# A Strassen down product, with weights stationary, in an RWKV-7 and MLP kernel

## The chip, the cores and the metric

The kernel runs on one core of one Trainium2 chip. The metric is the device time of one execution in microseconds (us). TensorE (PE) does the matmuls, VectorE (DVE), ScalarE (ACT) and GpSimd (POOL) the elementwise work, and SyncE (SP) issues all DMAs. Everything is float32.

## The reference

A recurrence over 768 steps for 4 batches and 8 heads of 40 channels, and behind it an MLP over the 3072 tokens:

```python
for t in range(S):                                   # S = 768, state is 40 x 40 for each (batch, head)
    y[:, :, t] = einsum('bhd,bhde->bhe', rt, state)
    Sa = einsum('bhde,bhe->bhd', state, at)
    state = state * wt[:, :, None, :] - einsum('bhd,bhe->bhde', Sa, bt) + einsum('bhd,bhe->bhde', vt, kt)
x = y.transpose(0, 2, 1, 3).reshape(3072, 320)
h = x @ w_in                                         # 320 x 2048
g = h * (1.0 / (1.0 + exp(-1.702 * h)))
out = g @ w_out                                      # 2048 x 320
```

## The kernel before

**The recurrence.** Time is cut into 12 chunks of 64 steps. A *unit* is one chunk of one pair of batches, so there are 24 units, and units 2c and 2c+1 make up chunk c. For each unit the kernel loads its tiles (`load`, `load_w`), forms decays (`decay`), scales the inputs and forms score products (`prep`: ps_A, ps_RV), inverts the triangular matrix of the chunk in levels (`inverse`: ps_N, ps_level, ps_Q, ps_T) and applies it to state and inputs (`solve`: ps_zT, ps_rz, ps_B, ps_X, ps_y). The last product of a unit is `read` (ps_y). From it come the new state and the output y, on VectorE, and then x = y times a decay (`decayed`, four steps on DVE or POOL). x goes to DRAM (`part_with`, x_dram<-x) and is read back in another layout, twice, into both halves of the partitions (`get_back`, xT_all<-x_dram). All of these DMAs are issued on SP, in the order of the list below.

**The MLP**, `mlp(c)`, works on the 256 tokens of one chunk. TensorE is used as four 64x64 tiles (`QUARTERS`), so four matmuls run at once; I call them a set. In the *up* product the weights are stationary and 256 tokens move: 40 sets for a chunk, eight groups of 256 features with 5 steps of 64 over the 320 inputs each. Four Gelus of 128x1024 (ACT) turn them into g. In the *down* product g is stationary and 320 columns of w_out move:

```python
for r, b in QUARTERS:
    o = p * 128 + b * 64
    mm(po[HALF[b], r, :DM], g[HALF[r], f % 2, o:o + 64], w_out_sb[HALF[r], f * DM:(f + 1) * DM], f == 0)
```

That is 32 sets for a chunk, in two accumulations of 128 tokens. Each one is copied to the tile ob (ACT or DVE), the sum of the other half of the rows is added (DVE), and two DMAs store 64 tokens each. w_in and w_out come as int64 bit patterns, 1.3 MB for each of eight pieces (`weight`), and are turned into floats on ACT, DVE and POOL (`joined`, 3 us each). `raws` says where the raw pieces stand before that: in the tile `extra`, in free parts of w_sb, or in the part of xT_all that chunks 1 and 2 use later.

**The order.** Nothing is scheduled by a tool at build time. The program makes a list of tasks with what each reads and writes (`plan.add`), and `ORDER`, a string, names each task by its number, with a letter for its engine (p, a, d, g, s) and a digit for its pair of PSUM banks. Every engine works through its tasks strictly in this order, and so does SP with the DMAs. A matmul that waits holds up all matmuls behind it. The figures in `plan.add`, such as `{"POOL": 730.0, "DVE": 434.0}`, are estimates that don't reach the chip. Line 300 is the helper `mm` that issues every matmul, so that in the profile matmuls are told apart by their tile.

**Buffers that matter here.** Tiles go round: `g` has four of 128 x 1024, xT_all has three chunks (`c % 3`), and all MLP and recurrence products share four pairs of PSUM banks.

Of the kernel before, what the change touches and what calls it, by code (L numbers as in the profile page):

```python
# [16 lines left out]
FP32 = mybir.dt.float32  # L17
# [89 lines left out]
ORDER = """  # L107
0s 8s 26s 5s 7s 9s 3a 6s 87p0 88p1 24s 89a1 1s 2s 12s 102a 95d 100p2 90a0 93d 158a 101d2 98p3 96g 10s 94d 17s 97g 16s 99d3
103p1 4a 11s 132p0 104a1 105d1 142p2 143p3 133a0 106d 130p1 14s 144a3 13s 107p0 15s 18s 151g 108a0 109d0 51s 131a1 110p3 27s
149g 150d 111a3 112d3 159p0 156p1 145a2 161d0 160a0 152g 113p3 345s 92a 162d 25s 153d 114a3 163p2 42s 115d3 34s 19a 274s 264p0  # L110
165d2 265p3 164a2 22d 266a3 166p2 20d 273s 21d 33s 43s 167a2 154p3 168d2 23g 35s 28a 157d1 116p2 155d3 169p1 117a2 118d2 267a0
279d 63s 280g 119p3 277s 171d1 36s 44s 123a3 120d3 343s 125d3 121a 278g 124d3 29d 287a 126p2 170a1 288p0 127a2 30d 172p1 479s
122a3 31d 289a0 128p2 54s 173a1 45s 129d2 32g 62s 174d1 134p3 37a 290d0 175p2 344s 135d3 180a2 146s 178a2 275s 176d2 136p1
179a2 38d 181a2 39d 177a 282g 276s 291d 91s 138a1 182p0 188p3 281d 183a0 186p2 139d 137a1 283p0 187a2 184p1 189a3 40d 140s
292p2 46a 60s 284d0 41g 285p3 185d1 148a 286d3 190p0 293a2 294d2 334p1 335p3 357a 191d0 141s 268g 147s 336a3 315d 192p2 47d
337a1 348d 316p0 194a2 346s 295p3 349d 61s 317a0 195g 347s 358p1 296a3 297d3 360d1 318a0 298p3 271a 361d 319p0 338g 300d3 196s
193a2 320a0 355p2 385d 270s 48d 299a3 362p0 356d2 351g 301p3 363a0 364d0 350g 386p2 197s 302d3 365p0 387a2 269s 352g 359a1
303d3 388a2 323p1 367d0 366a0 321p3 49d 324a1 304p2 322a3 478s 325d1 50g 353p0 309a2 470p3 354d0 209p1 307a2 210p1 310a2 305d2
211p1 308a2 272d 198p0 341a 199p0 72s 212p1 70s 64a 200p0 340s 368p2 52s 342d 339s 69s 201p0 369a2 202p0 370d2 203p0 471a
213p1 65d 214p1 389p2 66d 472a3 483g 204p0 390a2 560s 371p3 67d 306a 53s 215p1 71s 482s 216p1 372a3 217p1 476a 220p2 373d3 68g  # L120
218p1 221p2 477d 219a1 205p0 222p2 206p0 223p2 224p2 78s 559s 207p0 55a 311p3 225p2 79s 312d3 80s 226p2 208a0 58d 313p1 374p3
314d1 227p2 56d 379a3 228p2 229p2 57d 326p0 230a2 59g 393p1 327d0 378a3 391p2 394a1 375d3 231p0 558s 392d2 376a 232p0 233p0
395d1 81s 73a 234p0 480s 381p2 235p0 474s 328p1 475s 382a2 74d 377a3 485d 380a3 236p0 75d 481s 492a 242p2 486d 243p2 82a 76d
484d 77g 383p3 237p0 384d3 244p2 329d1 330d1 488p3 473d 238p0 531d 245p2 487g 246p2 489d3 85d 532p1 708s 239p0 533a1 396p3
331d 534a1 240p0 247p2 397d3 332s 241a0 562s 535p1 83d 490p3 536a1 84d 398p0 706s 572a 491d3 86g 550p1 253p3 399d0 551a 555s
400d0 561s 333s 254p3 401d 255p3 552a1 564d 493p0 402s 556a 567g 570p1 554s 494d0 248p2 705s 563d 566g 249p2 495d0 498d 256p3
571d1 565g 403s 250a2 496a0 251d2 696p1 497g 557d 539p0 252s 537p2 257p3 538a2 704s 540d0 701s 258p3 553d 611d 697a 499d 573p2
259p3 576a2 574d2 784s 710d 700s 260p3 787s 541d0 575d2 404p0 578d 261a3 577g 405p0 579d 698a1 568p2 711g 500p1 406p0 569d2
501a1 407p0 262d3 580p2 702a 502d1 263s 408p0 582d2 409p0 503d 410p0 583d 504a 612p3 411p0 584g 613d3 412p0 614d3 413p0 505p1
709d 414a0 426p3 506d1 427p3 428p3 507d1 429p3 699d 581d2 430p3 615p1 703d 431p3 616a1 785s 585p0 432p3 508d 586a0 433p3 587d0  # L130
434p3 509a 588d 435p3 589d 448p2 436a3 510p1 590p0 511a1 449p2 592d0 591a0 512d1 415p3 513d 416p3 593d 514a 417p3 594g 418p3
515p0 419p3 516a0 517d0 595p1 518d 420p3 596a1 597d1 421p3 598d 422p3 519a 599d 423p3 424p3 520p0 425a3 437p1 521d0 438p1
523d0 522g 439p1 524d0 440p1 525d0 441p1 442p1 526d0 527p3 718p0 528a3 443p1 719d0 929s 444p1 720d0 529p3 445p1 721d0 446p1
530d3 600p0 723d 447a1 542p3 722d 724g 603d0 605a0 619p1 604d0 543d3 450p2 620a1 606d0 544p3 621d1 601d0 602d 617p1 707s 546d3
451p2 618a1 783s 712d 547g 713d 607p0 725p1 608a0 452p2 609p0 453p2 548s 610d0 932s 454p2 727d1 726d1 622p0 728d 545d3 729a
775p1 455p2 623d0 780s 776a 549s 756d 730p3 624p0 456d2 457d2 731d3 458s 459p2 777a1 778g 732d3 786s 788g 781a 779s 626d0
460p2 625d0 627g 733d 795p1 835d 734a 461p2 735p3 791g 462p2 628s 736a3 796d1 737d3 716p0 792g 738d 463p2 782d 739g 1011s
920p1 757p3 925s 464p2 717d0 758a3 629s 759a3 790d 465p2 740p0 789d 466p2 741a0 742d0 921a 797p3 467d2 760p0 1008s 468d2 800a3
923d 652p2 469s 761d0 922a1 653p2 926a 930s 798d3 714p1 799d3 654p2 924s 802d 801g 655p2 934d 803a 656p2 836p0 657p2 715d1
658p2 659p2 837d0 762p3 838d0 927d 660p2 763a3 661p2 764p1 662a2 743d 630p0 744d 928s 631p0 632p0 765d1 804p3 766d1 633p0  # L140
805a3 806d3 634p0 807d 635p0 808a 745p2 636p0 748d2 637p0 749d2 839p1 933g 750d2 638p0 840a1 1009s 751d2 639p0 809p3 746d2
935g 640a0 641p1 810d3 642p1 793p2 747a 811d3 674p0 812d 794d2 813a 752p3 643p1 753a3 814p2 644p1 815a2 816d2 754p3 645p1
755d3 646p1 817d 647p1 818a 767p2 841p3 768d2 648p1 842a3 649p1 819p2 650p1 820a2 821d2 769p3 822d 651a1 823d 675p0 771d3 931s
770d3 772g 824p2 936d 676p0 827a2 828a2 942p1 829a2 677p0 1153s 830a2 937d 945a1 773s 663p3 825d2 664p3 943d1 1156s 826a 665p3
944d1 999p2 947d 946g 666p3 1000a 1004s 980d 940p1 948g 667p3 941d1 668p3 774s 669p3 670p3 831p1 671p3 1001a2 1002d 1003s
832d1 672p3 1005a 1013d 678p0 673a3 1006d 833p2 843p1 679p0 834d2 1007s 844d1 938p2 845d1 680p0 939d2 846p3 681p0 847d3 949p1
1012g 682d0 848p2 950a1 683d0 1014d 684s 685p3 849d2 1015g 1010s 850d2 1021p0 1016g 951d1 686p3 1024a0 1232s 851d 1235s 981p2
687p3 982a2 952d 852s 1022d0 983a2 953g 1144p1 1023d0 688p3 1026d 1145a 1149s 1025d 1027g 984p2 1059d 689p3 1154s 954p0 853s
985a2 1147g 690p3 1158d 1148s 955a0 956d0 986p2 1146a1 957d 1150a 691p3 958d 987a2 1151d 988p0 692p3 989a0 1152s 990d0 959p1
693a3 865p2 960a1 694d3 866p2 961d1 867p2 695s 962d 868p2 963d 1028p0 869p2 1029a0 1030d0 870p2 1031d 1157g 871p2 1159d 1032a  # L150
1060p3 872p2 873p2 1061a3 874p2 1062d3 1033p1 875a2 854p0 1035d1 855p0 1036d 856p0 1037d 1063p3 857p0 1064d3 1034a1 858p0
964p2 859p0 965a2 966d2 1038p1 967d 860p0 1039a1 1040d1 861p0 1041d 1017p3 968a 1042g 862p0 1018d3 863p0 969p2 864a0 876p1
970d2 877p1 972d2 971g 1043p3 973d2 878p1 1044a3 974d2 879p1 975d2 880p1 881p1 1045d3 1019p0 1046d 976p2 1047a 882p1 1020d0
1233s 883p1 977a2 1166p3 884p1 1169a3 1167d3 1377s 978p0 885p1 1168d3 898p2 1171d 1170g 886a1 979d0 887p3 1172a 1048p0 991p1
1051a0 888p3 1052a0 992d1 889p3 1053a0 890p3 1054a0 891p3 1049d0 993p1 1050a 1067p0 994d1 1160g 1155s 892p3 1161d 1068a0 893p3
894p3 1069d0 1380s 895p3 1204d 1065p0 995d1 896p3 996d 1066a0 1231s 1055p1 899p2 897a3 1056d1 997s 1173p0 1223p3 900p2 1174a0
1175d0 1228s 1176d 1224a 1177g 1057p1 901p2 1058d1 1070p0 998s 1164p1 1225a3 1226d 1236g 1227s 1071d0 902p2 1229a 1165d1
1162p3 903p2 1238d 1163d3 904p2 1237d 1178p0 1230d 905p2 1179a0 1180d0 1245p1 906a2 1181d 1072p3 1248a1 1456s 907d2 1182g
1246d1 908s 1247d1 909p0 1250d 1234s 1239g 1073d3 1251a 910p0 1240g 1074d3 1249d 1183p2 1459s 1283d 1368p1 911p0 1184a2 1075d
1373s 912p0 1185d2 1369a 1076s 1186d 1252p3 1187d 913p0 1370a1 1371g 1372s 1382d 1253a3 1188p2 1254d3 1374a 914p0 1255d 1190d2  # L160
1256g 1077s 1189a2 1191d 1243p1 1375d 915p0 1192g 1257p3 916p0 1244d1 1258a3 1259d3 1205p2 917d0 1206a2 1193p1 918d0 1207a2
# [86 lines left out]
@with_exitstack  # L248
def rwkv7_gelu_quick(ctx: ExitStack, tc: tile.TileContext, time_d, v_d, w_d, wc_d, ak_d, b_d, rv_d, w_in, w_out, out):
    nc = tc.nc  # L250
    H, D, S = 8, 40, out.shape[0] // 4
    DM = H * D
    C = 64
    MID = C // 2
# [875 lines left out]
```

## Time and profile before

| what | before |
|---|---|
| time, median of 3 runs (lowest, highest) | 677.54 us (677.51, 680.37) |
| the profiled execution: its own time, first to last instruction (span) | 681.1 us |
| PE busy | 652.0 us, 96% |
| DVE busy | 445.5 us, 65% |
| ACT busy | 330.7 us, 49% |
| POOL busy | 176.7 us, 26% |
| ps_up, ps_down: share of the chain that ended last | 31%, 30% |
| DMA | 69.73 MB, 102 GB/s |
| PE clock granted, mean | 0.990 |

The page has no time for the profiled execution but its span, which therefore stands for it. *Busy* is the time in which an engine has at least one instruction in progress; loading of weights (PEld) runs beside the matmuls (PE). The chain that ended last is followed back from the last instruction, step by step, to what each step waited for. A float32 matmul leaves two records, so that a set of four matmuls is eight records.

### The profile page before, as it was taken

Reading aid. Unit: us, or ns where it says so; the run is one execution under the profiler, and the core shown is the slowest. Engines: PE = TensorE matmul, PEld = TensorE weight load, DVE = VectorE, ACT = ScalarE, POOL = GpSimd, SP = SyncE. Lnnn points to the kernel's source line nnn. Section 1 sums busy time; section 2 is a strip of 40 time slices with the busy share of each in tenths; the row PEclk is TensorE's granted clock in tenths of the full one; section 3 lists DMA queues with packets and bytes.
Section 4 is the critical chain, followed back from the end, with each engine's and each line's share of the span. In section 5 each row is a group of like instructions: output and inputs, shape, how many; then the busy total and the mean of one; then the engine's idle time right before and its main releaser. Section 6 shows DMA issues by size and latency. Waiting matters only on the chain.

```text
span 681.1 us, 42181 instructions
## 1 busy us (share of the span) xinstructions
PE 652.0 (96%) x19488; PEld 572.4 (84%) x19488; DVE 445.5 (65%) x906; ACT 330.7 (49%) x688; POOL 176.7 (26%) x204
## 2 busy tenths in 40 slices
PE   5777999999999999999999999999999999999997
PEld 5667888997987788888888898899899799889996
DVE  4687877777867668767776587868556766675001
ACT  4675845544564654664545445455454354252110
POOL 5443444225123123123123211321412421300000
PEclk9788999999999999999999999999999999999999
DMA  7874755205314314432404413513502312200100
GB/s 235 275 244 148 228 158 173 89 14 155 108 50 139 103 45 125 124 108 67 121 23 131 140 34 107 154 33 106 149 29 71 121 51 58 58 13 23 51 12 21
DMA packets 35312, 69.73 MB, mean 102 GB/s; under 512 B 5440, under 2 KB 14656, under 8 KB 35136
## 3 DMA queue, kind: packets, MB, share of 16 engines
q1 hardware_dynamic: 35136, 67.03, 32.8%
q8 instruction: 153, 2.51, 1.6%
q14 instruction: 23, 0.19, 0.1%
HBM read 59.15 MB, written 7.86 MB: 98 GB/s over the span
## 4 chain that ended last, share of the span: by engine, by line
PE 91%; DMA 4%; ACT 1%; DVE 1%; issue 1%; SPq 0%; ACTq 0%; DVEq 0%
PE ps_up L300 31%; PE ps_down L300 30%; PE ps_level L300 9%; PE ps_y L300 5%; PE ps_B L300 4%; PE ps_X L300 2%; PE ps_N L300 2%; PE ps_rz L300 2%; PE ps_RV L300 2%; PE ps_A L300 1%; DMA ak<-in_ak 1%; PE ps_zT L300 1%; PE ps_Q L300 1%; DMA time<-in_time 1%; PE ps_T L300 1%
## 5 line engine op out<-in xcount | busy, mean ns | idle before, releaser
L300 PE MATMUL ps_up<-xT_all,w_sb 64*64 64x256 f32 x3840 | 254.4, 377 | 2.0 <-DMA xT_all<-x_dram 1.1
L300 PE MATMUL ps_down<-w_sb,g 64*64 64x320 f32 x3072 | 240.3, 430 | 1.1 <-issue 0.9
L300 PEld LDWEIGHTS ps_up<-xT_all,w_sb 64*64 64x64 f32 x3840 | 172.9, 133 | 17.7 <-issue 2.5
L300 PEld LDWEIGHTS ps_down<-w_sb,g 64*64 64x64 f32 x3072 | 143.3, 133 | 31.4 <-issue 1.6
L988 ACT ACTIVATE g<-ps_up 128x1024 f32<-128x1024 f32 x48 | 49.1, 1024 | 44.7 <-PE ps_up L300 44.3
L709 POOL TENSOR_TENSOR EX<-ES,quads 128x512 f32<-128x512 f32 x29 | 38.3, 1323 | 115.5 <-DVE ES L702 83.1
L751 ACT COPY W<-ps_level 128x512 f32<-128x512 f32 x56 | 32.7, 585 | 69.1 <-PE ps_level L300 67.4
L300 PEld LDWEIGHTS ps_level<-W,EX 64*64 64x64 f32 x2560 | 59.2, 134 | 5.8 <-DVE T L830 0.2
L300 PE MATMUL ps_level<-W,EX 64*64 64x64 f32 (+1 forms) x2560 | 56.2, 217 | 0.0
L753 DVE TENSOR_TENSOR E<-two,ps_level 128x256 f32<-128x256 f32 x80 | 33.1, 415 | 34.7 <-ACT W L751 30.7
L707 ACT ACTIVATE EX<-ES,quads 128x256 f32<-128x256 f32 x80 | 36.3, 501 | 30.4 <-DVE ES L702 29.9
L619 POOL TENSOR_TENSOR ak<-ak,FT 128x512 f32<-128x512 f32 x16 | 22.0, 1378 | 76.2 <-DMA ak<-in_ak 54.4
L300 PE MATMUL ps_level<-PT,EX 64*64 64x64 f32 (+2 forms) x1280 | 34.9, 244 | 5.7 <-DVE EX L723 4.8
L300 PEld LDWEIGHTS ps_level<-PT,EX 64*64 64x64 f32 x1280 | 32.6, 145 | 8.9 <-DVE EX L723 5.7
L702 DVE STREAM_TRANSPOSE ES<-E 128x256 f32<-128x256 f32 x80 | 35.2, 442 | 4.7 <-DVE E L753 0.5
L300 PE MATMUL ps_y<-M,bh 64*64 64x104 f32 (+1 forms) x768 | 34.8, 247 | 1.3 <-DVE M L907 0.8
L300 PE MATMUL ps_y<-RV,kh 64*64 64x104 f32 (+1 forms) x768 | 34.9, 247 | 0.3 <-DVE EX L723 0.3
L891 ACT COPY B<-ps_B 128x416 f32<-128x416 f32 (+1 forms) x34 | 16.5, 492 | 33.5 <-PE ps_B L300 33.2
L300 PEld LDWEIGHTS ps_y<-RV,kh 64*64 64x64 f32 x768 | 28.9, 133 | 2.0 <-DVE M L907 0.5
L907 DVE TENSOR_TENSOR M<-ps_X,later 128x832 f32<-128x832 f32 (+1 forms) x24 | 23.8, 993 | 9.8 <-PE ps_X L300 9.5
L627 POOL TENSOR_TENSOR kh<-time,G 128x320 f32<-128x320 f32 x18 | 16.2, 902 | 48.4 <-PE ps_y L300 34.4
L300 PEld LDWEIGHTS ps_y<-M,bh 64*64 64x64 f32 x768 | 27.0, 133 | 1.9 <-DVE M L907 1.2
(131 smaller groups left out, 1097.2 us busy)
## 6 DMA issues: line engine op xcount, KB each, us to landing
ak<-in_ak SPq DMA_DIRECT2D x48, 160.0 KB
rv<-in_rv SPq DMA_DIRECT2D x48, 160.0 KB
time<-in_time SPq DMA_DIRECT2D x24, 320.0 KB
xT_all<-x_dram SPq DMA_DIRECT2D x48, 160.0 KB
wc<-in_wc SPq DMA_DIRECT2D x20, 264.0 KB
logw<-in_w SPq DMA_DIRECT2D x24, 160.0 KB
RV<-in_v SPq DMA_DIRECT2D x24, 160.0 KB
b<-in_b SPq DMA_DIRECT2D x48, 80.0 KB
```

Of the source, the lines that this page charges most:

```text
L300: nc.tensor.matmul(o, lhsT, rhs, start=start, stop=True, skip_group_check=True)
L619: plan.add(R, {"DVE": 690.0, "POOL": 1270.0, "sbuf": True}, lambda t: of(t.engine).tensor_mul(ahT(), ahT(), FT_of(i)), reads=T("ak", "FT") ...
L627: plan.add(R + 4, {"POOL": 870.0, "DVE": 490.0, "sbuf": True}, lambda t, n=n, dst=dst: of(t.engine).tensor_mul(dst(i)[:, :, :D], by_head(t ...
L702: plan.add(rank, dve(256), lambda t: nc.vector.transpose(ES(n), source(t)), writes=[key("ES", n, 6)], **reads)
L707: nc.scalar.activation(dst[:, :, h], ES(n), ACT.Copy, scale=quads[:, h, :1])
L709: of(t.engine).tensor_mul(dst, ES(n).unsqueeze(2).to_broadcast([128, 8, 2, 32]), quads.unsqueeze(1).to_broadcast([128, 8, 2, 32]))
L751: plan.add(rank, any2(512), lambda t: copy(t.engine)(tiles_of(W(n + 1)), blocks(psum(t, ""), 64)), writes=[key("W", n + 1, 5)], pair=pair)
L753: plan.add(rank, dve(256), lambda t: nc.vector.tensor_sub(tiles_of(E(n + 1)), every(two32, [128, 2, 4, 32]), blocks(psum(t, ""), 64)[:, :, ...
L891: plan.add(R, any2(4 * wide), lambda t: copy(t.engine)(dst(), some(psum(t, "")[:, :, :208])), writes=[("Bv", i)] if x and c > 0 else T("B" ...
L907: plan.add(R + 1, dve(8 * wide), lambda t: nc.vector.tensor_tensor(M_of(i)[:, :, :wide].rearrange("p (j b) n -> p b j n", b=2), some(psum( ...
L988: plan.add(-45, {"ACT": 1030.0, "table": "gelu"}, lambda t: nc.scalar.activation(g_of(c * NQ + q).rearrange("p m r n -> p r m n"), psum(t, ...
```

## The change

**Chunks go in pairs.** `GROUPS` makes chunks 0 and 1 single and the others five pairs: (2,3), (4,5), (6,7), (8,9), (10,11). A single chunk (`single_chunk`) keeps its up product. Its down product has the weights stationary and 256 tokens moving (32 sets of 256, and 16 sets of 128 for the last 64 of the 320 outputs).

**The up product of a pair** (`two_chunks`) moves the 512 tokens of both chunks at once, 40 sets for a pair, but for pairs (2,3) and (4,5) (`SPLIT`), which take one chunk after the other with 256 tokens, and Gelus of half the size.

**The down product of a pair.** Of the 320 outputs 256 are halved into two blocks of 128 (`OF`), the 2048 features are two halves (j), and the two chunks are two blocks of 256 tokens. For this product of 2x2 blocks seven products of a block are formed rather than eight, by Strassen's scheme in Winograd's form: four new blocks of weights S1 to S4 (`forms`, made once, on POOL and DVE, in 16 steps; S1 in place of X21), four mixed blocks of g for each of eight feature groups (`mix`: T13, T2, T4, 24 steps for a pair, in place, on DVE or POOL), and sums of products (`combine`, 7 steps for a pair, on tiles of 128x256). The last 64 outputs (`of_five`) are done as plain products. The sets have 256 moving columns throughout. The products of a pair come in four phases: X11 and X12 with the plain g; the last 64 outputs and S4; S1 and S2 with mixed g; S3 and X22 with mixed g. A phase gathers two products of 128x256 at once: a copy and an add of 512 (`gather`).

**Buffers.** g has eight tiles of 128 x 1024, which one pair fills. A g tile can be written again only when the last phase of the pair before has read it. xT_all keeps three chunks, with a new assignment (`X_SLOT`). The six result tiles a to f stand in `extra`, free once all weights are made.

**The output** is stored transposed, as (12 x 320) x 256, by DMAs of up to 128 rows of 1 KB, and put in place on the host after the launch. `dynamic_dma_scratch_size=1024` shrinks a reserve in SBUF.

**The order** is a new list throughout, 2830 tasks for 2700. It begins `102a 0s 7s 6s 8s 5s 3a` for `0s 8s 26s 5s 7s 9s 3a`: the first weight piece, 26s before, now comes behind the loads of units 0 and 1.

The diff, without the order and with the core of each function:

```diff
+    GROUPS = [(0,), (1,), (2, 3), (4, 5), (6, 7), (8, 9), (10, 11)]
+    RING = 8
+    SPLIT = (2,3)
+    X_SLOT = [0, 1, 2, 1, 0, 1, 2, 1, 0, 1, 2, 1]
...
+    X11, X12, X21, X22 = (w_of[:, :, j, i * OF:(i + 1) * OF] for i, j in product(BITS, BITS))
+    S1 = X21
...
+    def forms():
+        for name, dst, a, b, op, reads in (("S3", S3, X11, X21, ALU.subtract, done),
+                                           ("S2", S2, X22, S3, ALU.subtract, [("S3", 0)]),
+                                           ("S4", S4, X12, S2, ALU.subtract, [("S2", 0)]),
+                                           ("S1", S1, X21, X22, ALU.add, [("S2", 0)] + ...
...
-                        for r, b in QUARTERS:
-                            o = p * 128 + b * 64
-                            mm(po[HALF[b], r, :DM], g[HALF[r], f % 2, o:o + 64], w_out_sb[HALF[r], f * DM:(f + 1) * DM], f == 0)
...
+    def single_chunk(g):
...
+                        for r, h in QUARTERS:
+                            o = f * DM + i * OF + h * 64
+                            mm(po[HALF[h], r, i * 256:(i + 1) * 256], w_out_sb[HALF[r], o:o + 64], g_of(n)[HALF[r], f % 4], f == 0 and i == 0)
...
+    def two_chunks(g):
...
+                for r, h in QUARTERS:
+                    mm(ph[HALF[h], r], w_in_sb[HALF[r], m, k, h * 64:(h + 1) * 64], x_all[HALF[r], :, :, k], k == 0)
+            plan.add(R + m, pe((1, 512)), go, reads=[("xs", (c, p)) for c in (a, b) for p in BITS] + [("weight", m // 2)],
+                     uses=[x_key(a), x_key(b)], room=[("g", base + m)], pair=pair, most=1)
...
+        def mix(m):
...
+                    ("T13", 512, lambda: G()[:, 0:2], lambda: G()[:, 0:4:3], lambda: G()[:, 1:2].to_broadcast([128, 2, 256]), ALU.subtract, ...
+                    ("T2", 256, lambda: G()[:, 3], lambda: G()[:, 3], lambda: G()[:, 0], ALU.add, [("T13", n)]),
+                    ("T4", 256, lambda: G()[:, 2], lambda: G()[:, 2], lambda: G()[:, 3], ALU.subtract, [("T2", n)])):
...
+        phase("b", "c", two_of((X11, 0), (X12, 2), ...), 10)
+        combine("c", "b", ALU.add)
+        phase("a", "d", fifth_and_three, 20)
+        phase("e", "f", two_of((S1, 0), (S2, 3), ...), 30)
+        combine("b", "f", ALU.add)
+        combine("d", "e", ALU.subtract)
+        combine("d", "b", ALU.add)
+        phase("a", "c", two_of((S3, 1), (X22, 2), ...), 40)
+        combine("b", "a", ALU.add)
+        combine("c", "b", ALU.add)
...
-    nc = bacc.Bacc("TRN2", target_bir_lowering=False, num_devices=1)
+    nc = bacc.Bacc("TRN2", target_bir_lowering=False, num_devices=1, dynamic_dma_scratch_size=1024)
-    out = nc.dram_tensor("out", (n_tokens, d_out), FP32, kind="ExternalOutput").ap()
+    out = nc.dram_tensor("out", (NC * d_out, B * C), FP32, kind="ExternalOutput").ap()
```

More of the change, by code (lines that the diff above doesn't have):

```diff
@@ new lines, in combine, with store @@
+    def combine(x, y, op):
+        reads = [now(x), now(y)]
+        plan.add(-45, {"POOL": 730.0, "DVE": 434.0, "sbuf": True}, lambda t: of(t.engine).tensor_tensor(
+            out=place(x), in0=place(x), in1=place(y), op=op), reads=reads, writes=[new(x)])
+    def store(k, parts):
+        size = sum(dst.shape[0] * dst.shape[1] for dst, _ in parts)
+        plan.add(-100, {"SP": 350.0 * len(parts)}, lambda t: [nc.sync.dma_start(dst, src) for dst, src in parts], reads=[now(k)], size=4 * size)
@@ L1026, in rwkv7_gelu_quick, with mlp @@
+    def mlp(g):
+        if len(GROUPS[g]) == 2 and (g == 0 or len(GROUPS[g - 1]) == 1):
+            forms()
+        (two_chunks if len(GROUPS[g]) == 2 else single_chunk)(g)
     for i in range(3):
@@ L1043, in rwkv7_gelu_quick @@
         solve(i)
-        if i % 2:
-            mlp(i // 2)
+        for g in range(len(GROUPS)):
+            if i == 2 * GROUPS[g][-1] + 1:
+                mlp(g)
     tasks = plan.listed(ORDER)
```

480 lines of the change are left out of this document (303 added, 177 removed).

## The prediction

> **What bounds the kernel now.** I read the page first, then the chain of waits, then busy time by stretch. The page:
>
> ```profile
> span 681.1 us, 42181 instructions
> PE 652.0 (96%) x19488; PEld 572.4 (84%) x19488; DVE 445.5 (65%) x906; ACT 330.7 (49%) x688; POOL 176.7 (26%) x204
> PE   5777999999999999999999999999999999999997
> PE 91%; DMA 4%; ACT 1%; DVE 1%; issue 1%; SPq 0%; ACTq 0%; DVEq 0%
> ```
>
> The chain that ends last runs on TensorE for 91% of the span, and TensorE is short of work only in the first four slices (68 us). So time comes off where TensorE gets less to do, as long as nothing new makes it wait. The chain's tail gives the price of a product:
>
> ```profile
> 628.81 10.77 PE ps_down L300 x158
> 639.58 4.32 PE ps_up L300 x80
> 662.23 14.02 PE ps_down L300 x208
> ```
>
> A matmul leaves two records and four 64x64 matmuls run at once, so a set of four is eight records. 80 up records are 10 sets: 0.432 us a set with 256 moving columns. Down records come at 16 in 1.08 us all through the chain: 0.540 us a set with 320 columns. Both are 1.69 ns a column: the price is columns alone.
>
> VectorE stands close behind. Two steady stretches of the windows view (columns: stretch, length, busy us and instructions of PE, PEld, DVE, ACT, POOL, clock, DMA share, GB/s):
>
> ```profile
> 269.00:322.00 53.00, 53.00 (x1672) 44.57 (x1667) 38.52 (x79) 30.29 (x60) 15.11 (x15) 1.00 0.36 104
> 425.00:442.00 17.00, 17.00 (x487) 13.64 (x482) 14.57 (x29) 6.82 (x16) 6.45 (x6) 1.00 0.54 155
> ```
>
> Over a pair of units VectorE is 73% busy; the best 17 us slice with TensorE full has it at 86%. The third thing to see is the trip of x through DRAM, which ahead of chunk 8 shows on the chain:
>
> ```profile
> 484.07 4.06 DMA x_dram<-x
> 488.74 4.43 DMA xT_all<-x_dram
> 493.21 2.88 PE ps_up L300 x49
> ```
>
> **The trip's length.** Unit 23's last read product ends at 628.81; VectorE forms y (0.69 us) and x (0.9), SyncE issues the write at 630.51, 1.7 after the product, and the read back at 635.36; the first up product starts at 639.58. That is 10.8 us, all under down products. From write issue to read issue the timeline has 2.2 us (625.88 to 628.05) to 4.5 (483.72 to 488.21); from read issue to up product 4.2 (here) to 5.0 (488.21 to 493.21). So a trip is 8.1 to 11.2 us, 9.7 in the middle.
>
> **The change, part by part.** The sum is against the profiled execution, 681.1 us, which is 3.6 above the median of the runs, 677.54; I take 3.6 off at the end. Half a percent (3.4 us) is about what a measurement of this kernel can tell from no change.
>
> *Down products.* Removed: 12 chunks x 32 sets x 0.540 = 207.4 us. Added: for each of five pairs 7 x 8 = 56 sets of Strassen's products and 16 sets for the last 64 outputs, 72 x 0.432 = 31.1, together 155.5; for chunks 0 and 1, 32 x 0.432 and 16 sets of 128 columns at 0.216, 17.3 each, 34.6. Sum 190.1: **-17.3 us**, all on the chain.
>
> *Up products.* Three pairs take 512 columns a set: 40 sets for 80. No row has 512 columns; by 1.69 ns a column a set is 0.864, the same time. Bounds: 0.85, if a fixed part is saved, and 0.88: -2 to +2 us over 120 sets. I take **0**, since 256 and 320 columns have one price.
>
> *Work beside TensorE.* Counting the engine letters in the new order: 120 mixing steps on g (51 DVE, 69 POOL), 35 combining steps (12, 23), 16 for the weight forms (4, 12). By rows: 512 elements cost 0.69 (DVE) or 1.28 (POOL), 256 cost 0.44 or 0.73. DVE: 16 x 0.69 + 51 x 0.44 = 33; POOL: 24 x 1.28 + 80 x 0.73 = 89. Gathering takes 22 adds of 512 at 0.68 and 8 copies at 0.68 for 24 adds and 9 copies of 320 at 0.49: +5 on DVE. Other steps change engine (x goes to POOL 16 times for 10), so priced entry by entry VectorE comes to 490 us from 445, POOL to 275 from 177; ScalarE stays at 330. None is the chain on average, so the price is **0** while TensorE has other work queued; without that cover a late mixing step costs its own length, 0.4 to 1.3 us. The cover is thinnest from unit 5's y to unit 15's: there the new order holds 220 us of TensorE and 208 of VectorE, 95%, against 73 to 79% in the old.
>
> *The x trip.* This is the wait that the change adds. A pair's up product needs both chunks, its g buffers are freed only by the previous pair's last phase, and nothing else of the product is left to queue. Summing the TensorE entries between an odd unit's y and the first up product of its chunk, the old order has 12.0 to 15.0 us for chunks 2 to 10 and 10.8 for 11. The new one has 10.2 (chunk 1), 9.5, 7.0, 25.7, 7.9 (2 to 5), 7.6 (6 and 7), 7.0 (8 and 9), 6.1 (10 and 11). Against a trip of 9.7 these are short by 0, 0.2, 2.7, 0, 1.8, 2.1, 2.7, 3.6: **+13.1 us**; a trip of 8.1 gives 4.9, one of 11.2 gives 23.1. TensorE takes its queue in order, so behind a waiting up product stand the recurrence's own next products, and VectorE waits for those. I take the middle, since the issues of write and read in the timeline lie 2.2 to 4.7 us apart all through the run.
>
> *The start.* The order is new there too. Unit 1's score needs its a and b tiles, and in the old list 3.94 MB are issued up to them, weights among them; they end on the chain:
>
> ```profile
> 9.61 7.07 DMA ak<-in_ak
> 16.69 3.91 DMA extra<-in_w_in
> ```
>
> The new list has 2.46 MB ahead of the same point and all weights behind. 1.48 MB at the 235 to 275 GB/s of the first slices is 5.4 to 6.3 us. Up to unit 3's y both lists load the same (22.4 MB for 22.1), so it may be given back: between 0 and -6.3, **-4.5** taken, as the first two units need no weight.
>
> *The end.* Now a copy and an add of 320 (0.49 each) and two stores follow the last product, 4.9 us in all. Then: a copy (0.59) and an add (0.69) of 512, two combining steps (0.44 and 0.73 on POOL), two stores: 1.5 us more steps, less 0.4 as the stores go out one after the other: **+1.1**.
>
> Sum: 681.1 - 17.3 - 4.5 + 13.1 + 1.1 = 673.5; less 3.6: **670 us**.
>
> **Rivals.**
>
> *The trips stay covered.* The fill is a sum of work; where VectorE makes it last longer, or the write lands in 2.2 us as at 625.88, no up product waits. For: chunk 4 has 25.7 us, and at the end no loads are in flight. Against: four fills are 7.6 or less, under the shortest trip. 681.1 - 17.3 - 6.3 + 1.1 - 3.6 = 655 us.
>
> *VectorE becomes the bound between unit 5's and unit 15's y: slower.* If it can be kept busy at 86% at most, the best slice above, its 208 us last 242, 22 more than TensorE's 220. With the trips behind it (2.1 + 2.7 + 3.6) 681.1 - 17.3 - 4.5 + 22 + 8.4 + 1.1 - 3.6 = 687.2. It decides against the change once waits in the middle pass 17.3 + 4.5 - 1.1 = 20.7 us. For: 95% has no precedent in this trace once loading is over. Against: TensorE lost nothing at 86%. What could bring VectorE there is seen in two rows, 128x512 steps of the same kind on POOL and DVE (min, median, max ns):
>
> ```profile
> L709 DVE TENSOR_TENSOR EX<-ES,quads x31: 649/691/845, 117.2 to 613.6; 128x512 f32<-128x512 f32 x31
> L709 POOL TENSOR_TENSOR EX<-ES,quads x29: 1272/1280/1679, 126.2 to 599.7; 128x512 f32<-128x512 f32 x29
> ```
>
> The longest ran 0.15 and 0.40 us over their medians. With some 80 VectorE steps of two SBUF inputs in the stretch at 0.1 us more each, 208 becomes 216 and the 86% case 251: 9 us dearer, 696. [...]
>
> *The sets do not go at column price.* If 256 columns with weights stationary cost 0.540 a set, as with 320, down would take 238 us: 718. The up sets already run so at 0.432.
>
> **From cases to numbers.** Forecast 0.50: over its trips, and with the start given back or not, 660 to 684, of which 0.32 is faster (below 674.1), 0.15 same and 0.03 slower (above 680.9). Trips covered 0.20. VectorE the bound 0.27, of which 0.01 within the half percent, if it reaches 90%. Column price 0.03. Faster 0.32 + 0.20 = 0.52, same 0.16, slower 0.03 + 0.26 + 0.03 = 0.32. The range goes from just above the covered trips to the VectorE case, 656 to 688.
>
> **What would show it.** In the profile after: down sets of 256 columns at 0.43 us and PE busy near 635; waits of ps_up on the DMA of xT_all, 1 to 4 us each, at five chunk boundaries; first y some 5 us earlier; VectorE at about 490 us, and above 86% in slices 10 to 24. Wrong would be waits of TensorE on the mixing steps (ps_down behind g), or a first score no earlier than 20 us.

## The result and the profile after

The changed kernel takes **738.23 us** (median of 4 runs, 735.42 to 740.59) against 677.52 for the kernel before on the same chip: 1.088 times as long, 95% interval 1.083 to 1.093. An execution more than 1.5% above the fastest of its kernel counts as slow, and all ratios are taken from the others alone, so a ratio can differ from the quotient of two medians. The profiled execution took 739.62 us, with a span of 737.9. The page:

```profile
span 737.9 us, 41517 instructions
PE 665.5 (90%) x19104; PEld 521.5 (71%) x19104; DVE 517.3 (70%) x966; ACT 312.9 (42%) x683; POOL 281.6 (38%) x326
PE   4786789899888999898997998999989999989996
PEclk9888999999999999999997999999999999999999
PE 17%; issue 3%; POOL 2%; DMA 2%; DVE 2%; SPq 0%; POOLq 0%; ACT 0%; DVEq 0%; ACTq 0%
```

TensorE's row has eights and sevens all through the middle, where it was full before. The chain tells little here, as it could be followed over a quarter of the span only. The two traces are best compared in three stretches, cut where the last read product (ps_y) of unit 5 ends and where that of unit 23 ends. I call these ends y5 and y23. The windows view, first of before, then of after (stretch, length, busy us and instructions of PE, PEld, DVE, ACT, POOL, clock, DMA share, GB/s):

```profile
0.00:162.30 162.30, 140.06 (x4356) 123.51 (x4360) 116.43 (x210) 93.95 (x211) 63.90 (x83) 0.96 0.56 173
162.30:628.80 466.50, 464.47 (x14374) 402.07 (x14370) 324.57 (x686) 231.86 (x472) 112.79 (x122) 1.00 0.30 86
628.80:681.10 52.30, 47.42 (x770) 46.86 (x760) 4.52 (x11) 4.94 (x6) 0.00 (x0) 1.00 0.11 30
```

```profile
0.00:181.00 181.00, 145.62 (x4580) 125.75 (x4584) 141.85 (x215) 87.31 (x196) 74.00 (x96) 0.94 0.49 155
181.00:655.10 474.10, 446.06 (x13524) 345.28 (x13520) 357.53 (x722) 215.12 (x475) 190.46 (x212) 0.98 0.28 83
655.10:737.90 82.80, 73.81 (x1008) 50.43 (x1000) 17.91 (x30) 10.43 (x12) 17.13 (x19) 0.97 0.08 26
```

The difference of 56.8 us between the spans is +18.7 in the start, +7.6 in the middle and +30.5 in the tail. Beside it stands TensorE's work, each record priced at what it takes in a full queue of before (0.054 us at 256 columns, 0.067 at 320, the recurrence's shapes by their own rows; 0.108 at 512 is an estimate from the first two):

| stretch | before: length, PE work | after: length, PE work | change of length, of work |
|---|---|---|---|
| start to y5 | 162.3, 123.2 | 181.0, 126.4 | +18.7, +3.2 |
| y5 to y23 | 466.5, 461.3 | 474.1, 416.4 | +7.6, -44.9 |
| y23 to the end | 52.3, 47.1 | 82.8, 71.5 | +30.5, +24.4 |

The saving is there: the work sums to 631.6 and 614.3, 17.3 less, as forecast to the tenth. The prices are the forecast's own, so the agreement says that the products are as many as counted; that the price holds too is seen in a row of the chain behind y23, 20 sets of 256 columns at 0.441 us each, where 0.432 was forecast:

```profile
704.44 8.82 PE ps_down L309 x160
```

But 44.9 us are missing in the middle, where the time does not follow, and 24.4 us have been moved behind y23, where it does. Two questions follow: what paces the middle if TensorE doesn't, and what happened in the start.

### The profile page after: what moved, and what is told of

Read it like the earlier page. It is cut to its first block, busy times and chain, and to the rows that moved or that the text cites. A ratio compares the mean times of both kernels' runs of the same rounds, so it can differ in the third digit from the quotient of the medians.

```text
span 737.9 us, 41517 instructions
## 1 busy us (share of the span) xinstructions
PE 665.5 (90%) x19104; PEld 521.5 (71%) x19104; DVE 517.3 (70%) x966; ACT 312.9 (42%) x683; POOL 281.6 (38%) x326
## 5 line engine op out<-in xcount | busy, mean ns | idle before, releaser
L309 PE MATMUL ps_up<-xT_all,w_sb 64*64 64x256 f32 (+1 forms) x2880 | 251.4, 455 | 8.7 <-DMA xT_all<-x_dram 4.9
L309 PE MATMUL ps_down<-g,w_sb 64*64 64x256 f32 (+1 forms) x2688 | 180.6, 368 | 1.7 <-issue 1.4
L309 PEld LDWEIGHTS ps_up<-xT_all,w_sb 64*64 64x64 f32 x2880 | 121.8, 135 | 60.0 <-issue 38.3
L309 PEld LDWEIGHTS ps_down<-g,w_sb 64*64 64x64 f32 x2688 | 113.3, 134 | 22.0 <-issue 2.8
L1125 POOL TENSOR_TENSOR g<-g 128x256 f32<-128x256 f32 (+1 forms) x69 | 71.9, 1064 | 27.3 <-PE ps_down L309 20.1
L309 PE MATMUL ps_down<-g,extra 64*64 64x256 f32 x960 | 81.6, 376 | 0.0
L981 POOL TENSOR_TENSOR x<-zr,FT 128x128 f32<-128x128 f32 x64 | 33.2, 549 | 50.4 <-DVE zr L971 42.6
L1158 ACT ACTIVATE g<-ps_up 128x1024 f32<-128x1024 f32 x24 | 24.6, 1025 | 65.4 <-PE ps_up L309 65.3
L309 PEld LDWEIGHTS ps_down<-g,extra 64*64 64x64 f32 x960 | 42.6, 133 | 7.2 <-DVE g L1125 0.2
L1125 DVE TENSOR_TENSOR g<-g 128x256 f32<-128x256 f32 (+1 forms) x51 | 36.4, 736 | 4.3 <-POOL g L1125 2.7
```

What stands on the lines that cost most here:

```text
L309: nc.tensor.matmul(o, lhsT, rhs, start=start, stop=True, skip_group_check=True)
L981: of(t.engine).tensor_mul(x[:, b ^ u, b], both(i)[:, at, :64], FT_of(i)[:, at])
L1125: plan.add(-44, {"POOL": 180.0 + 2.14 * size, "DVE": 170.0 + 1.03 * size, "sbuf": True}, lambda t, dst=dst, x=x, y=y, op=op: of(t.engine). ...
L1158: plan.add(-45, {"ACT": 1030.0, "table": "gelu"}, lambda t, m=m: nc.scalar.activation(g_of(base + m).rearrange("p (r k) n -> p r (k n)", r ...
```

## Experiments

Ratios are to the kernel before on the same chip, whose median was 677.5 to 682.2 in the various sets. The expectations' figures for VectorE (346, 391, 358 and so on) are sums of the steps' durations, which overlap a little; the window rows here count each moment once, and are 6 to 9% lower.

**e1, no mixing steps.**

```diff
-  lambda t, ...: of(t.engine).tensor_tensor(out=dst(), in0=x(), in1=y(), op=op), ...   # in mix(m)
+  lambda t: None, ...
```

> The new kernel took 738 us, 61 more than the one before, though TensorE has 17 us less to do. This run leaves out the 120 mixing steps (the three steps on each g buffer), so products 3 to 7 work on unmixed g; all products, gathers, combining steps, trips of x and the order stay. Theory A: the mixing steps cost the time, because they take VectorE and GpSimd and lengthen the recurrence's own steps there. Then the excess of VectorE's durations over each group's tenth percentile falls from 70 to about 35 us, VectorE's busy time from 517 to some 440 us, and the time to 675 to 700 us. Theory B: the trips of x cost it, in that ps_up waits longer: no change beyond 3 us, 735 to 741. Theory C: the new order by itself costs it, since it queues the recurrence later, whatever the steps between do: above 720 us.

Measured: 726.18 us, ratio 1.066 (1.061 to 1.071). Of the 8.8% only 2.2 go, about 15 us (12 by the medians). Theory A alone falls, C holds. The middle, in a window from y5 to y23:

```profile
181.10:647.60 466.50, 443.57 (x13531) 345.11 (x13523) 328.65 (x685) 215.41 (x475) 128.67 (x154) 0.99 0.29 85
```

It takes what the kernel before takes, to the tenth, with VectorE at 329 us (325 before) and 45 us less work for TensorE.

**e2, mixing steps of 8 columns.**

```diff
-  out=dst(), in0=x(), in1=y()
+  out=dst()[..., :8], in0=x()[..., :8], in1=y()[..., :8]
```

> All mixing steps stay in their places in both queues, with their waits, but work on 8 columns instead of 256 or 512 (the rest of g stays unmixed). If it is the length of the mixing steps that costs (time on the engines and lock of one engine by the other), this is within 10 us of the run without mixing. If it is their waits (a mixing step that waits for GELU or for product 2 holds the steps of the recurrence queued behind it), the time stays above 720 us.

Measured: 726.74 us, ratio 1.067 (1.060 to 1.074), the same as without. So what mixing costs is the steps' length, and nothing is lost by their waits. (The mark of 720 us decides nothing, since e1 itself lies above it.)

**e3, up products that wait for no x.**

```diff
-  x_all[HALF[r], :, :, k]
+  x_fix[HALF[r], :, k * 256:(k + 1) * 256]      # x_fix = w_sb[:, :2560]
```

> The up products of the five pairs read a fixed piece of w_sb as their moving matrix and so wait for no x (part of the computation is changed: the pairs' output no longer depends on x); the trips of x themselves stay, as do all lengths. Theory B (trips of x): 713 to 725 us, the 13 to 25 us that ps_up loses. Theory A: the waits only move, as VectorE is late anyway: 732 to 741 us.

Measured: 733.17 us, ratio 1.077 (1.072 to 1.081). The trips cost 5 us, 7 by the ratio, less than the 13 that I had counted: theory B falls as the main cause.

**e4, all mixing on VectorE.**

```diff
+  plan.tasks[-1].moved = "DVE"
...
-  t.engine, t.bank = e, int(bank or 0)
+  t.engine, t.bank = getattr(t, "moved", e), int(bank or 0)
```

> All 120 mixing steps run on VectorE, in the same place of the order, instead of 51 there and 69 on GpSimd; nothing else differs. VectorE gains some 69 x 0.5 = 35 us of work, GpSimd loses 72. If the two engines excluding each other is the larger part of the cost, VectorE's own steps get shorter and the time falls, to 715 to 735 us. If VectorE's load is the larger part, the time rises to 745 to 770 us.

Measured: 745.43 us, ratio 1.092 (1.086 to 1.097): no faster. It is 7 us slower by the medians, but the ratio of the changed kernel is 1.088 (1.083 to 1.093), so that neither of the two forecasts is clearly met. The longer steps beside GpSimd are there all the same. The same step in the changed kernel, where GpSimd mixes beside, and here (groups by shape: busy us, mean ns, idle before):

```profile
L1125 DVE TENSOR_TENSOR g<-g 128x256 f32<-128x256 f32 x35 | 21.9, 643 | 3.0 <-POOL g L1125 2.7 <-PE ps_down L309 0.2
```

```profile
L1125 DVE TENSOR_TENSOR g<-g 128x256 f32<-128x256 f32 x80 | 35.4, 466 | 0.9 <-PE ps_down L309 0.2
```

VectorE's step falls from 643 to 466 ns when GpSimd stops mixing. That costs the changed kernel some 6 us of VectorE's time over 35 steps. The time, which does not fall, shows that this is not what decides here.

**e5 and e6, few products**, in the kernels after and before. This is the cut that separates TensorE's load from the recurrence.

```diff
-  for r, h in QUARTERS:
+  for r, h in QUARTERS if k == 0 else ():       # up; in the down product: if m == 0 (f == 0)
```

> Without mixing the new kernel still takes 726 us; between unit 5's and unit 23's last read product it takes 466.5 us, exactly as the kernel before (466.5), though TensorE has some 45 us less to do there. Here each up product keeps one of its five steps over channels and each down product one of its eight steps over g, so TensorE loses some 330 us of its work; every other instruction, the order, the trips and the mixing stay (most of the product is left out). Theory D: the recurrence (its chain through TensorE, VectorE, ScalarE and GpSimd in this order of the queues) paces the middle, whatever TensorE does beside it: the stretch from y5 to y23 stays above 430 us of 474. Rival: TensorE's work and its waits pace it: the stretch falls under 380 us.

> The same cut in the kernel before (one of five steps of each up product, one of sixteen hidden slices of each down product). By theory D its recurrence has hardly less to do than the new kernel's, so this stretch takes 400 to 450 us of 466, a little below the new one's. If the new order or the new steps on VectorE and GpSimd slow the recurrence itself, it is shorter than in the cut new kernel by 30 us or more.

Measured: 710.88 us, ratio 1.042 (1.035 to 1.049), and 601.04 us, ratio 0.881 (0.874 to 0.888). The two middles, e5 first:

```profile
180.20:662.80 482.60, 334.17 (x9928) 268.26 (x9928) 357.19 (x722) 214.12 (x474) 189.81 (x212) 0.72 0.27 81
```

```profile
158.90:578.00 419.10, 302.07 (x9972) 245.95 (x9968) 320.36 (x687) 229.01 (x477) 113.83 (x123) 0.80 0.33 95
```

In e5 more than half of TensorE's work is taken out of the middle (416 to 198 us), and the middle grows by 8.5 us; what is won, 36.6 us, is won in the tail (82.8 to 46.2). In e6 TensorE loses 266 us and the middle falls by 47. So theory D's forecast is met: after the change, less work for TensorE no longer shortens the middle. Before, the recurrence had 42 us in hand under TensorE's 461. What the expectation of e6 calls the alternative is met as well: with few products the new middle is 63 us longer than the old.

Two reservations. The clock falls to 0.72 and 0.80 here, and the recurrence's own products get longer with it: a product of 64x64 that levels the triangular matrix (ps_level from W and EX) takes 278 ns in the mean in e5's middle and 261 in e6's, 223 in the changed kernel's and 218 before. At full clock both recurrences would presumably need less than 483 and 419 us; how much less, no run shows, so it is not shown that the recurrence has nothing in hand in the changed kernel as it runs. And in the kernels with all products whose chain can be followed to the start (e1, e2, e4, e8, e11 to e14) TensorE still carries 60 to 81% of the chain, for 91% before. The two take turns; it is not a clean change from one pacer to the other.

**e7 and e8, weights prepared on 8 columns; e8 also without mixing and with fixed x.**

```diff
-  nc.gpsimd.tensor_tensor(out=scale(), in0=scale(), in1=word(INT32, 1), op=ALU.add)
+  nc.gpsimd.tensor_tensor(out=scale()[:, :8], in0=scale()[:, :8], in1=word(INT32, 1)[:, :8], op=ALU.add)
```

(and the same in the three VectorE steps ahead of it)

> In the new kernel unit 3's last read product ends at 121.6 us, against 107.4 before, and between units 1 and 3 VectorE is busy for 61.5 us against 42.4, with the preparation of the weights (four steps on each of eight pieces, the last on GpSimd for 2.9 us) now in that stretch. Here these four steps work on 8 of 1280 columns (the weights are not finished); loads, order and everything else stay. If this preparation is what costs the 14 us there, y3 comes at 105 to 111 us and the time falls to 722 to 728 us. If it is the late loads or the order, y3 stays above 117 us and the time within 5 us of 738.

> Three of the suspects are taken away at once in the new kernel: no mixing steps (12 us alone), weights prepared on 8 columns only, and the pairs' up products read a fixed piece of w_sb and wait for no x (5 us alone). If the costs are separate, 738 - 12 - 5 - 14 = 707 us. What remains above the 677 of before then comes from none of them: by theory D from the last pair's product, all of which lies behind the last read product of unit 23 (83 us from there to the end, against 52 before), while the stretch before it stays at 450 to 466 us. If the waits hang together, so that one late step is enough to hold the rest, the gain is larger than the sum: under 695 us.

Measured: e7 732.54 us, but its executions lay between 717 and 737 with the mean clock between 0.992 and 0.969, so its time settles little; in its profile y3 ends at 111.3 us (121.6 in the changed kernel) and y5 at 170.3. e8 took 708.47 us, ratio 1.042 (1.037 to 1.047), 1.5 us off the 707 foretold for separate costs, of which the 14 for the weights were assumed. Its y5 comes at 170.3 too, against 181.1 in e1, which has the whole preparation: 10.8 us. What it does is seen in e1's chain of waits (start, us, what):

```profile
75.60 1.47 DVE w_sb L460 x2
77.07 1.45 DVE w_sb L464 x2
78.51 0.54 issue
79.06 2.88 DVE wc L560
81.93 1.21 DVE wc L561
83.14 0.72 DVE extra L468
83.86 0.62 DVE EX L751
84.49 2.80 DVE bh L655
...
95.66 3.31 DVE wc L561
```

From 75 to 100 us the chain is VectorE: the weights' steps (L460 to L468), and between them steps of the next unit's decays that take 2.8 to 3.3 us where their group's tenth percentile is 0.5 to 0.7. Beside them GpSimd runs the last step of a weight, 2.9 to 3.5 us long. In the changed kernel six VectorE steps run more than 1.5 us over their group's tenth percentile, in the kernel before one. Each of them stands beside such a GpSimd step, and in e7, where that step takes 0.2 to 0.5 us, there is none.

**e9 and e10, few products without mixing; e10 also without the adds of `gather` and all of `combine`.** The edits are those of e5 and e1, and

```diff
-  lambda t: nc.vector.tensor_add(dst(), dst(), got(t, 1))
+  lambda t: None
```

> With 330 us of TensorE's work cut away, the new kernel still took 711 us and the one before 601; from y5 to y23 482.6 and 418.9 us, with VectorE busy for 391 (81%) and 346 us (83%). Theory E: the recurrence paces the middle and VectorE paces the recurrence; it can be kept busy at some 82% of the time only, as its steps wait for one another's results. Here the cut new kernel also loses its 120 mixing steps. Theory E: VectorE's 358 us in that stretch at 82% are 437 us, and the time falls from 711 to 655 to 675 us. Rival, the new order itself: the queues are arranged so that the recurrence takes longer whatever is between; then the stretch stays above 465 us and the time above 690.

> As the run before it, and the adds behind the gather copies and all combining steps of the outputs are left out as well (24 adds of 512 or 128 columns on VectorE, 35 steps on VectorE and GpSimd). VectorE then has some 338 us from y5 to y23, less than the cut kernel before with 346. Theory E: that stretch takes 410 to 425 us, the same as there (418.9), and the time 630 to 650 us. The order as cause: it stays above 440 us.

Measured: 685.41 us, ratio 1.004 (1.001 to 1.008), and 679.47 us, ratio 0.992 (0.988 to 0.996). The middle, e9 first:

```profile
184.30:647.40 463.10, 324.09 (x9928) 259.46 (x9928) 329.52 (x685) 213.07 (x471) 129.52 (x154) 0.75 0.29 84
```

```profile
185.10:647.30 462.20, 326.72 (x9928) 265.26 (x9928) 316.10 (x660) 213.06 (x472) 116.70 (x138) 0.73 0.29 84
```

Theory E falls, though e9 just misses the marks of its rival as well (465 and 690 us). With hardly a new step left (three of the weight forms, 3 us, and the copies of `gather`), VectorE is busy for less than in e6 (316 us to 320) and GpSimd for about as much, and the stretch takes 43 us more. What is left is the list, that is, the order of the steps together with the engine that each is given. Its mark is in VectorE's waits in the middle, of e6 and then of e10 (what waits, for what: us in total, times, longest):

```profile
DVE E L753 <- ACT W L751: 24.2, 22, 3.9
DVE B L891 <- PE ps_B L300: 6.3, 6, 2.1
DVE zraw L934 <- PE ps_y L300: 6.3, 7, 1.8
DVE M L907 <- PE ps_X L300: 6.1, 7, 1.5
```

```profile
DVE E L781 <- PE ps_level L309: 22.4, 20, 2.8
DVE T L858 <- PE ps_T L309: 15.0, 12, 3.5
DVE M L935 <- PE ps_X L309: 14.9, 11, 2.5
DVE zr L971 <- PE ps_y L309: 13.0, 9, 3.2
DVE A L666 <- PE ps_A L309: 11.3, 10, 2.2
```

Summed over all such rows, VectorE waits 40 us for TensorE's results in e6 and 117 in e10, though TensorE is busy for 71 to 72% of both; for ScalarE's it waits 43 and 23. That the product that VectorE needs stands behind another that waits for VectorE or ScalarE in turn is how I read this; the sums do not show it step by step.

**e11 and e12, all products, no mixing, adds or combining; e12 also with short weights and fixed x.**

> The new kernel with all its products, without mixing, adds and combining steps. VectorE then has some 338 us from y5 to y23, TensorE its 416 us. If either of them sets the pace alone, that stretch falls to 420 to 440 us from 466.5 (without mixing) and the time to 685 to 700 us. If the list, which fixes how many products lie between two steps of the recurrence on TensorE's queue, makes the two add up, the stretch stays at 450 to 465 us and the time at 712 to 725.

> All the suspects left out at once in the new kernel: mixing, adds, combining, the weights' preparation on 8 of 1280 columns, and up products of the pairs that wait for no x. The run that kept only adds and combining took 708 us. If nothing is left but the order and the last pair's product behind y23, the stretch from y5 to y23 is 440 to 460 us and the time 690 to 705 us, above the 677 of the kernel before although it does less than that in every engine; if the steps themselves were the whole cost, it is below 665 us.

Measured: 725.16 us, ratio 1.065 (1.061 to 1.068), and 706.72 us, ratio 1.038 (1.033 to 1.042). Adds and combining cost nothing that shows (e1 took 1.066, e8 1.042). e12, e8's equal, has its middle at 456 us:

```profile
171.40:627.60 456.20, 435.75 (x13525) 341.92 (x13521) 315.01 (x660) 215.55 (x475) 116.92 (x138) 0.99 0.29 87
```

With every suspect step gone the kernel still takes 3.8% more than before. e11's middle of 460.6 us lies where the expectation puts a sum of VectorE's and TensorE's work. But e10 takes 462 with 198 us of work for TensorE in place of 416, if at a clock of 0.73, so a plain sum it is not either. e12's chain says where the time lies:

```profile
PE 81%; DVE 8%; issue 4%; ACT 3%; DMA 3%; SPq 0%; DVEq 0%; ACTq 0%
```

It leaves TensorE more often than before the change (91%), though every engine has less to do.

**e13 and e14, another list.** Nothing but the `ORDER` text changes. In e13 the 1908 shared tasks stand as in the kernel before, on each engine, in e14 as in the one after; the product's 922 tasks are placed by one rule.

```diff
-ORDER = """102a 0s 7s 6s 8s 5s 3a ...
+ORDER = """...
```

> The whole new computation with another ORDER text and nothing else. With few products, no mixing and no adds the recurrence alone still took 679 us in the new order against 601 in the old one, at the same busy time of VectorE (345 and 346 us from y5 to y23, in 462 and 419 us): the new order itself is the cost. Here all 1908 tasks that the two kernels share (loads, weights, recurrence) stand on each engine in the order of the kernel before and on the engine they had there, except that the two transfers of each x go out as soon as they can; the 922 tasks of the product (up, GELU, mixing, forms, down, gathering, stores) are put in where the engine would wait otherwise. Theory F (the recurrence's order costs the 50 us in start and middle, the last pair's product behind y23 the rest): y5 near 160 us, y23 near 610, and the time 680 to 705 us. Theory E (the added steps cost it wherever they stand): 720 us or more.

> The same rule for placing the product's tasks, but the shared tasks keep the order and engines of the new kernel. Theory F: y23 near 640 to 650 us and the time 715 to 735 us, 25 us or more above the run with the old order of the recurrence. If it was the placing of the product's tasks among the others that cost the time, this run comes within 10 us of the other.

Measured: 722.2 us, ratio 1.058 (1.051 to 1.065), and 754.13 us, ratio 1.109 (1.100 to 1.117). The recurrence's list, order and choice of engines together, is worth 32 us: the start ends at 168.5 in e13 and at 186.0 in e14, and the middles, e13 first, are

```profile
168.50:629.70 461.20, 429.58 (x13316) 342.93 (x13312) 352.61 (x724) 224.86 (x482) 171.72 (x181) 0.99 0.29 85
```

```profile
186.00:674.00 488.00, 443.87 (x13406) 345.74 (x13399) 351.61 (x709) 228.87 (x489) 180.44 (x206) 0.97 0.27 81
```

All products are in both and the clock is near full (0.99 and 0.97), so this is the cleanest measure of the order: 17.5 us in the start and 27 in the middle. But both times miss their forecasts: e13 is above its 680 to 705, e14 above its 715 to 735. e14 differs from the changed kernel by the places and engines of the product's tasks and of x's transfers alone and is 16 us slower, so those count too, and my rule is worse than the list that it replaced. It also leaves more behind y23, in e13 86 us of product, so that the tail takes 92.

**e15 and e16, what holds e13's middle.** e15 is another list, with some 40 us of the middle's VectorE steps moved to ScalarE. e16 is e13 with the cut of e5.

> The whole new computation, as in the run with the old order of the recurrence (722 us, 461 from y5 to y23), with two things changed in the ORDER text: steps that may run on either engine are moved from VectorE to ScalarE until VectorE has some 55 us less (about 455 us in all) and ScalarE 50 more, and the places of the steps are shifted a little where an engine would wait. If VectorE paces the recurrence in the old order, y5 to y23 falls to 425 to 440 us and the time to 675 to 695 us. If it is the order's waits of one engine for another, whatever VectorE's load, the stretch stays above 450 us and the time above 710.

> The run with the old order of the recurrence (722 us, 461 from y5 to y23), with one of five steps of each up product and one of eight of each down product, as in the earlier cuts. The kernel before takes 419 us there when cut so, the new one 483. If the new steps on VectorE and GpSimd lengthen the recurrence by themselves in the old order too, the stretch takes 440 to 465 us, and TensorE's products cost nothing on top. If in the old order the recurrence with them is as quick as before, it takes 415 to 430 us, and the 461 come from products and recurrence meeting on TensorE's queue.

Measured: 714.9 us (703.9 to 720.5), ratio 1.037 (1.028 to 1.047), and 637.74 us, ratio 0.936 (0.929 to 0.942). The middles, e15 first:

```profile
173.80:633.00 459.20, 438.99 (x13590) 351.03 (x13586) 311.16 (x632) 269.02 (x613) 162.72 (x180) 1.00 0.30 87
```

```profile
159.20:596.40 437.20, 307.24 (x9900) 245.56 (x9896) 357.05 (x723) 224.98 (x489) 176.53 (x186) 0.79 0.31 90
```

In e15 41 us less of VectorE's work took 2 us off the stretch of this profile. The profiled execution took 717.9 us, though, 6 and 14 more than the two that the ratio rests on, so its middle may be up to 14 us high; by the ratios (1.058 and 1.037) the whole gain is 14 us. So VectorE's load is not the only pacer, and most of what was taken from it was not won. The list was shifted in other places too, so even these 14 us are not VectorE's load alone. e16 falls below the range that I gave to the steps and above the one for the list, so both count. With the few-product runs the middle is a table of two by two:

| middle, few products | without the new steps | with them |
|---|---|---|
| old order of the recurrence | 419 (e6) | 437 (e16) |
| new order | 462 (e10) | 483 (e5) |

The new steps add 18 to 20 us to the recurrence, the new order 43 to 45, at the low clocks of these runs (0.80 and 0.79 in the upper row, 0.73 and 0.72 in the lower), so a part of what is put down to the order may be the clock; with all products e13 and e14 give the order 27 us. e16 also has my places for the product's tasks. VectorE's wait for TensorE, 40 us in e6, is 39 in e16, and 99 in e5: it belongs to the order.

No list tried here beats the kernel before.

## Why the prediction was wrong

The forecast was 670 us in a range of 656 to 688; 738 lies outside it.

- **Down products, -17.3 us "all on the chain".** This is the step that failed. The size was right to the tenth, the place was not. Of the middle 44.9 us were taken, and it became 7.6 longer. TensorE was the chain because before it had 461 us to do in a middle whose recurrence alone takes 419 (e6, at a clock of 0.80). So at most some 42 us and what the low clock hides could be won there, and the recurrence had itself become slower: by its order, 27 us with all products (e13 and e14) and 43 to 45 with few, and by the new steps, 12 to 15 us of the time with all products (e1) and 18 to 20 of the middle with few. TensorE's queue has been left waiting for it in between: 416 us of work in 474.
- **The end, +1.1 us.** It measured +30.5. I counted the steps behind the last product but not the product behind the last read: the pair (10,11) cannot start before y23. There are 1008 records of 71.5 us where 770 of 47.1 were; the trip of x (9.3 us from y23 to the first up product) and the last mixing steps make the rest (without the wait for x the tail takes 5.7 us less in e3, without mixing 3.1 less in e1). The entries in the list behind unit 23's read would have shown this beforehand, and I had summed such entries for the trips.
- **The start, -4.5 us.** Unit 1's first product of its a and b tiles (ps_N) did begin 2.3 us earlier (18.4 for 20.7 us), its ps_A 4.4 (24.8 for 29.2). By y1 it was given back (54.2 for 54.0), and y5 came 18.7 later. I had followed the bytes ahead of unit 1 and not the weights' preparation that is moved behind them: 18 of its 24 VectorE steps now lie between y1 and y3 (14 before), beside the decays, and the whole of it costs 10.8 us up to y5 (e1 and e8; what it cost before was not measured). With the old order y5 comes at 168.5 (e13), still 6 us behind the kernel before.
- **Extra work on VectorE and GpSimd, 0 us while hidden.** About 15 us for mixing (e1), none for the adds. VectorE came to 517 us, where 490 were forecast, and its steps grew longer: over each group's tenth percentile they add up to 70 us, 30 before.
- **The trips, +13.1 us.** The length was right (9.3 us at the end, 9.7 forecast), but ps_up waited for xT_all for 4.9 us in all (7 times, 3.3 the longest), and e3 puts the trips at 5 to 7 us, most of it in the tail (82.8 us with them, 77.1 without). Ahead of y23 TensorE waits for the recurrence anyway, and a trip is presumably paid only in part.
- **Up products, 0 us.** Held: in the longest row of them, 175 records of 512 columns start 0.106 us apart, where 0.108 was forecast.
- **The rivals.** "Trips covered" came true in its mechanism up to y23, where ps_up waits 1.6 us in all, but not behind it, and the time came out 83 us above its 655. The column price did not happen. "VectorE becomes the bound" had the right sign and the right place, but not the mechanism: VectorE is busy 75% of the middle, and 78% between unit 5's and unit 15's y, not 86%, and taking 41 us from it wins 14 at the most (e15). What delays it are waits on results. The 0.1 us a step that its dearer case added was an estimate that no run shows; the mixing step took 0.18 us more where GpSimd mixed too (643 ns for 466, e4).

Neither of the signs that I had named as wrong came: TensorE hardly waits on the mixing steps (0.2 us for ps_down in all), and unit 1's first product of a and b comes before 20 us. So these signs could not have caught the error. Of those named as right, the price of the down sets came and most others failed: the first y began 1.0 us later (43.1 for 42.1), VectorE came to 517 us, of the products' waits for xT_all one alone passed 1 us (3.3, behind y23), and PE was busy for 665 us where 635 were forecast. TensorE had some product in progress for 446 us of the middle, for 416 of work, and so looks busy in spite of its waits. What shows that the middle no longer follows TensorE's work are the lengths between the y.

**Still open:** which entries of the new list make TensorE and VectorE wait for each other; how much of the list's cost is the order of the steps and how much the choice of engines; what the recurrence alone needs at full clock; and why the middles of e13 and e15 stay at 459 to 461 us where the recurrence alone needs 437 (in e13) and TensorE's work is 405 and 420.

## What to carry to other kernels

Before work is taken off the engine that carries the chain, ask how much time the next chain has in hand: cut the first one's work in a run and see how far the time falls (here 47 us in the middle before, nothing after, with the clock to be read beside it: 0.72 to 0.80 in the middles with few products, 0.98 to 1.00 with all in the kernels before and after). Cut the span at the dependencies that no engine can pass (the last read product here) and sum the work in each piece: work that moves behind such a point is paid in full, and work saved ahead of it may be worth nothing. A hand-made order is a part of the kernel like any other, and a new one can cost more than the instructions that it was made for.

## What the runs showed of the hardware

TensorE's granted clock was lower in the runs with few products by more than I had thought. In the middle it was 1.00 and 0.98 with TensorE busy for 100% and 94% (before, after), and 0.72 to 0.80 with it busy for 69% to 72% (e5, e6, e9, e10, e16), though no single wait there is long (3.7 us at most in e6, 3.2 in e5 and e10). The products were slower there too: a ps_level product took 278 ns in e5's middle, 223 in the changed kernel's.

VectorE steps that ran beside a weight's last step on GpSimd (2.9 to 3.5 us) took longer in the changed kernel: the decays' scans, at 0.68 us in the tenth percentile, went up to 3.4 us. The six steps that ran more than 1.5 us over their group's tenth percentile each began during such a GpSimd step and ended 0.35 to 0.57 us behind its end; the longest, from 96.41 to 99.79 us, stood beside one from 95.88 to 99.22. With the weights' steps cut to 8 columns (e7) none of VectorE's steps was 1.5 us over its group's tenth percentile.
